# Performer attention with a gated MLP on one core: w_out loaded in eight pieces, and 120 scheduling priorities shifted by a search

## The chip, the core and the metric

The kernel runs on one core of one Trainium2 chip. The core has TensorE for matmuls ("PE" in the profile, and "PEld" for its weight loads), VectorE (DVE), ScalarE (ACT), GpSimd (POOL) and SyncE (SP), which here issues loads and stores. The metric is the device time of one execution in microseconds. An execution with a profile also has a span, from the first to the last instruction; in nearly all executions here the time is 1.8 to 2.1 us longer than the span.

## The reference, cut to what matters

```python
# q, k, v: (8 batches, 8 heads, 576 rows, 64) f32;  omega: (128, 64)
def phi(x):                                   # random features
    h = einsum('bhsd,md->bhsm', x, omega) - sum(x*x)/2
    return exp(h - max(h)) / sqrt(m)
kv  = einsum('bhsm,bhsd->bhmd', phi(k), v);  z = sum(phi(k), axis=2)
x   = einsum('bhsm,bhmd->bhsd', phi(q), kv) / (einsum(phi(q), z) + 1e-6)
x   = x as (4608, 512)
h   = x @ w_in                                # (512, 2048)
out = (h * clip(h + 3, 0, 6) / 6) @ w_out     # (2048, 512)
```

## The kernel before: the parts that the change touches

The kernel is written as a list of operations, each with a priority, the buffers it reads and writes, and an assumed duration on each engine that may do it. A list scheduler in the Python program plays this list against its own model of the core. Out of that come a fixed order of instructions for each engine, a choice of engine where there is one, and the semaphore waits. The chip keeps to this order (all 2233 weight loads stand in the same order in the three traces of the changed kernel), so an order that fits the model and not the chip costs time.

There are three stages. Attention of batch 0 runs alone (the "head"). Then TensorE does the first layer of block b beside the attention of batch b+1. The second layer of block b follows one block later. While TensorE has nothing to do in the head, dummy matmuls on a tile `fill` keep it busy.

```python
W_GATE = [("vl", 0)]*2+[("v32", 1, 3)]*2       # what each of four w_in loads waits for
...
def w_out_piece(g, gate):                      # four loads of 512 rows, cast to bf16 on the way
    op("POOL", 2.95, lambda E: E.dma_start(
        wo[:, 4 * g:4 * g + 4, :], w_out[512 * g:512 * g + 512, :].rearrange("(c p) e -> p c e", p=128)),
       -0.2 + 0.05 * g, reads=gate, writes=[("wo", g)], ...)
...
# scaling of the 64 leftover rows of v ("vcl"), one op for each half of the partitions;
# it reads the landed rows ("vl") and reciprocals of the first k maxima ("cc", "l")
op(EV_V if b else V0, {"POOL": 0.62, "DVE": dvet(260)}, ... E.tensor_tensor(vcl..., vl..., cc..., ALU.mult), ...)
...
# transposes on PE go to a PSUM bank of a ring of eight; a copy by DVE or ACT frees the bank
op("PE", len(dbl) * 0.057, e_T, p, reads=..., writes=[vT], alloc=[vT], ...)
op(EV_T if b else T0, both(n, 2), evac(... dst ..., ... vT ...), p, reads=[vT], writes=[(t + "T", x) for x in dbl])
...
def mm2(blk, tc):                              # second layer: 16 matmuls in groups of four
    for g in range(4):
        def e(E, g=g, ...):
            for f in range(4 * g, 4 * g + 4):
                ins = E.matmul(ring.t[vo.slot][...], gT[gu][:, f, 128 * tc:128 * tc + 128], wo[:, f, c0:c1], ...)
        op("PE", 4 * mmt(w), e, t, reads=[("gT", ...)...] + [("wo", g)], writes=[vo], alloc=[vo] if g == 0 else [], ...)
...
load(2, (), {"k": [("wo", 1)], "q": [("wo", 2)], "v": [("wo", 3)]})   # loads of batch 2 wait for w_out
```

The softmax here doesn't subtract the row's maximum and nothing guards it: scores larger than these inputs give would overflow.

## Time and profile before

The first three executions took 323.71 to 324.29 us, median 324.18. In rough numbers, of the profiled execution (span 321.8 us):

| stretch (us) | what PE does | lost there |
|---|---|---|
| 0 to 17.3 | head: attention of batch 0, 63 dummy matmuls | about 11.4 us |
| 17.3 to 38.95 | first layer of block 0, attention of batch 1 | about 0.3, before 18 us |
| 38.95 to 40.0 | changes over to the second layer | 0.6 to 0.7 |
| 40.0 to 318.8 | both layers, attention of later batches | 0 |
| 318.8 to 321.8 | last copy and store | not on PE |

"Lost" is PE's time that is not spent on real matmuls. Reading a trace in this way takes one more step than reading its busy shares, because a dummy is busy too. I take the weight loads in order of time and pair them with the program's own order of matmuls. Each matmul then counts for its start-to-start time at full rate in this trace (0.2158 us for 512 columns, 0.1093 for 256, 0.032 for 65, and so on), and a dummy counts for nothing. The loss at a moment is the time since the span's start minus the work done so far. Weight loads run ahead of their matmuls (by 0.21 us for most in this trace), so a value is good to about 0.15 us.

### The profile page before, as it was taken

How to read it: one execution, taken by the hardware profiler on the slowest of the kernel's cores; microseconds unless marked ns; L12 is line 12 of the kernel's file. 1: busy time of each engine (PE TensorE's matmuls, PEld its weight loads, DVE VectorE, ACT ScalarE, POOL GpSimd, SP SyncE). 2: the span in 40 equal slices, each digit the busy share in tenths (PEclk: the TensorE clock that was granted, in tenths of full speed). 3: DMA queues.
4: the chain of work that ended last, by engine and by line, in shares of the span. 5: the costliest groups of instructions: out<-in, count | busy, mean ns of one | idle time of the engine just before them, and what ended most of it. 6: DMA issues, size and time to landing. Idle time of an engine off the chain costs nothing.

```text
span 321.8 us, 5873 instructions
## 1 busy us (share of the span) xinstructions
PE 317.0 (98%) x2236; PEld 174.8 (54%) x2236; DVE 209.0 (65%) x460; ACT 189.1 (59%) x385; POOL 76.8 (24%) x107
## 2 busy tenths in 40 slices
PE   8999999999999999999999999999999999999996
PEld 6789855455654544565555545555555444444443
DVE  4988985597787947995796478846866353433411
ACT  3996982596595516966775387647674254344400
POOL 2765171065040600730333022402020000000000
DMA  7999999999940999897829963998012201000024
GB/s 249 269 201 204 236 146 234 225 184 170 226 122 34 136 173 271 99 196 118 236 31 188 191 208 39 183 201 224 16 50 67 73 27 41 33 35 33 33 67 98
DMA packets 91532, 44.79 MB, mean 139 GB/s; under 512 B 58096, under 2 KB 87024, under 8 KB 91504
## 3 DMA queue, kind: packets, MB, share of 16 engines
q1 hardware_dynamic: 64288, 31.31, 42.1%
q0 software_dynamic: 26512, 12.46, 31.4%
q10 hardware_dynamic: 704, 0.66, 0.6%
q8 instruction: 18, 0.29, 0.4%
q14 instruction: 10, 0.08, 0.1%
HBM read 36.73 MB, written 9.44 MB: 143 GB/s over the span
## 4 chain that ended last, share of the span: by engine, by line
PE 94%; DVE 4%; POOL 1%; issue 0%; ACT 0%; POOLq 0%; DVEq 0%
PE p L917 39%; PE p L859 34%; PE p L656 5%; PE p L639 4%; PE p L884 4%; PE p L791 3%; PE p L763 2%; DVE mx L648 2%; PE p L466 2%; PE p L429 1%; PE p L765 1%; POOL vc L750 0%; DVE vc L750 0%; DVE vcl L679 0%; DVE gT L895 0%
## 5 line engine op out<-in xcount | busy, mean ns | idle before, releaser
L917 PE MATMUL p<-wo,gT 128*128 128x512 bf16 (+2 forms) x592 | 141.0, 373 | 0.3 <-DVE qT L418 0.3
L867 DVE SCALAR_TENSOR_TENSOR gT<-tsb,p 128x512 bf16<-128x512 bf16 x128 | 86.8, 685 | 56.7 <-ACT tsb L865 56.1
L865 ACT ACTIVATE tsb<-p 128x512 bf16<-128x512 f32 x128 | 76.3, 601 | 71.1 <-PE p L859 70.6
L859 PE MATMUL p<-xT,wi 128*128 128x512 bf16 x448 | 107.3, 379 | 0.0
L917 PEld LDWEIGHTS p<-wo,gT 128*128 128x128 bf16 x592 | 56.1, 98 | 57.5 <-DVE qT L418 0.5
L859 PEld LDWEIGHTS p<-xT,wi 128*128 128x128 bf16 x448 | 42.6, 98 | 45.4
L648 DVE TENSOR_REDUCE mx<-kp 128x4 f32<-128x512 bf16 x72 | 46.7, 674 | 9.7 <-ACT kp L645 9.4
L645 ACT ACTIVATE kp<-p 128x512 bf16<-128x512 f32 x72 | 40.0, 619 | 15.1 <-PE p L639 15.1
L660 ACT ACTIVATE qpT<-p 128x512 bf16<-128x512 f32 (+1 forms) x80 | 41.4, 575 | 4.8 <-PE p L656 4.6
L750 POOL TENSOR_TENSOR vc<-v,cc 128x512 bf16<-128x512 f32 x22 | 23.4, 1064 | 36.3 <-DVE cc L746 27.0
L807 DVE TENSOR_TENSOR xb<-p,rec 128x384 bf16<-128x384 f32 (+1 forms) x64 | 28.5, 477 | 0.0
L639 PE MATMUL p<-om,kT 128*128 128x256 bf16 x144 | 23.0, 273 | 0.0
L656 PE MATMUL p<-qT,om 128*128 128x512 bf16 (+1 forms) x80 | 22.8, 358 | 0.0
L418 DVE COPY osb<-p 128x512 f32<-128x512 f32 (+2 forms) x12 | 7.8, 647 | 22.7 <-PE p L917 22.7
L417 ACT COPY osb<-p 128x512 f32<-128x512 f32 x25 | 14.8, 591 | 11.3 <-PE p L917 11.3
L500 POOL DMA_DIRECT2D k<-in_k_dram x12 | 9.1, 767 | 41.9 <-PE p L859 33.7
L639 PEld LDWEIGHTS p<-om,kT 128*128 128x128 bf16 x144 | 13.8, 98 | 9.7
L791 PEld LDWEIGHTS p<-kvz,qpT 128*128 128x128 bf16 x312 | 13.5, 98 | 5.8 <-ACT qpT L660 0.2
L859 PE MATMUL p<-xS,wi 128*128 128x512 bf16 x64 | 16.4, 379 | 0.0
L884 PE MATMUL p<-xT,wi 128*128 128x256 bf16 x128 | 15.9, 272 | 0.0
L763 PEld LDWEIGHTS p<-vc,kp 128*128 128x128 bf16 x256 | 11.9, 98 | 6.1 <-POOL vc L750 0.4
L791 PE MATMUL p<-kvz,qpT 128*128 128x65 bf16 x312 | 14.8, 194 | 0.0
(69 smaller groups left out, 215.9 us busy)
## 6 DMA issues: line engine op xcount, KB each, us to landing
out_dram<-osb SPq DMA_DIRECT2D x32, 256.0 KB, 2.6
v<-in_v_dram SPq DMA_DIRECT2D x14, 512.0 KB, 5.3
wi<-in_moe_w_in_dram POOLq DMA_DIRECT2D x4, 512.0 KB, 8.3
k<-in_k_dram POOLq DMA_DIRECT2D x8, 256.0 KB, 5.1
k<-in_q_dram POOLq DMA_DIRECT2D x8, 256.0 KB, 6.2
wo<-in_moe_w_out_dram POOLq DMA_DIRECT2D x4, 512.0 KB, 12.8
kb<-in_k_dram POOLq DMA_DIRECT2D x6, 256.0 KB, 5.3
qb<-in_q_dram POOLq DMA_DIRECT2D x6, 256.0 KB, 7.6
```

What stands on the lines that cost most here:

```text
L639: ins = E.matmul(ring.t[vK.slot][:, 256 * i:256 * i + 256], kT[:, 2 * u + i, :], om[:].rearrange("d t m -> d (t m)"), start=True, stop=True)
L645: op("ACT", actt(512), lambda E, u=u, vK=vK: E.activation(kp[pb][:, 4 * u:4 * u + 4, :].rearrange("p c m -> p (c m)"), ring.t[vK.slot], AF ...
L648: op("DVE", dvet(512), lambda E, u=u: E.reduce_max(mx[pb][:, 4 * u:4 * u + 4], kp[pb][:, 4 * u:4 * u + 4, :], axis=AX.X), pos(u) + 0.03, r ...
L656: op("PE", mmt(n), lambda E, vQ=vQ, lh=lh: E.matmul(ring.t[vQ.slot][:, 0:n], om[:, lh, :], src, start=True, stop=True), p + 0.045 * lh, re ...
L660: op("ACT", actt(n), lambda E, vQ=vQ, lh=lh: E.activation(dst(lh), ring.t[vQ.slot][:, 0:n].rearrange("m (j t) -> m j t", t=128), AF.Exp, s ...
L791: ins = E.matmul(d[:, hh, i - i0, :], qpT[pb][:, o:o + 128], kvz[m][:, 65 * hh:65 * hh + 65], start=True, stop=True)
L807: op("DVE", dvet(128 * n), lambda E: E.tensor_tensor(xv(i0, i1), psum()[:, :, :, 0:64], rbc, ALU.mult), t + 0.01, reads=[vn, ("rec", ru)], ...
L859: ins = E.matmul(ring.t[vh.slot], wi[:, c, 128 * f:128 * f + 128], xv[:, c, :], start=(c == 0), stop=(c == NJ - 1))
L865: op("ACT", actt(512), lambda E: E.activation(tsb[tu][:], ring.t[vh.slot], AF.Relu, bias=0.5, scale=1.0 / 6.0), t - 0.1, reads=[vh], write ...
L867: op("DVE", dvet(512), lambda E: E.scalar_tensor_tensor(gT[gu][:, f, :], tsb[tu][:], 1.0, ring.t[vh.slot], ALU.min, ALU.mult), t - 0.1, re ...
L884: ins = E.matmul(ring.t[vh.slot][:, 256 * g:256 * g + 256], wi[:, c, 128 * (f + g):128 * (f + g) + 128], xT[0][:, c, 256 * half:256 * half ...
L917: ins = E.matmul(ring.t[vo.slot][:, 0:c1 - c0], gT[gu][:, f, 128 * tc:128 * tc + 128], wo[:, f, c0:c1], start=(f == 0), stop=(f == NF - 1))
```

## The change

`URGENT` and `FIT` are two tolerances, in us, with which the scheduler picks the next instruction, and `NUDGE` is added to the priorities of the operations with these numbers. The intent is to let the second layer start on half a piece of w_out, and to find a better order of the first two batches by a search that shifts priorities and keeps what shortens the scheduler's own model.

```diff
-URGENT = 0.8
-FIT = 0.05
+URGENT = 0.5
+FIT = 0.1
+NUDGE = {
+    114: 0.0222, 119: 0.0169, 120: 0.0216, 122: 0.0313, 123: 0.0172, 124: -0.0176, 134: -0.0037, 137: 0.0668,
+    138: -0.1599, 142: -0.1553, 143: -0.0153, 145: 0.0442, 146: -0.0653, 147: -0.0395, 149: -0.042,
     ... (120 operations in all)
-    if idle and (not cand or idle[0][0] + (0.02 if idle[0][0] < 8.0 else idle[0][1].occ) <= m):
+    if idle and (not cand or idle[0][0] + (0.02 if idle[0][0] < 4.8 else 0.2 if idle[0][0] < 8.0 else idle[0][1].occ) <= m):
-    W_GATE = [("vl", 0)]*2+[("v32", 1, 3)]*2
+    W_GATE = [("q32", 1, 3)] * 4
+    WO = [(2 * i, 2 * i + 2) for i in range(8)]
     def w_out_piece(g, gate):
-        op("POOL", 2.95, lambda E: E.dma_start(
-            wo[:, 4 * g:4 * g + 4, :], w_out[512 * g:512 * g + 512, :].rearrange("(c p) e -> p c e", p=128)),
+        f0, f1 = WO[g]
+        op("POOL", 0.7375 * (f1 - f0), lambda E: E.dma_start(
+            wo[:, f0:f1, :], w_out[128 * f0:128 * f1, :].rearrange("(c p) e -> p c e", p=128)),
     ... (assumed GpSimd times of two scalings raised: 0.62 to 0.72, 1.2 to 1.32)
-            for g in range(4):
+            for f0, f1 in WO if blk == 0 else [(4 * g, 4 * g + 4) for g in range(4)]:
     ... (block 0 takes its second layer in groups of two matmuls, each waiting for its piece)
-            load(2, (), {"k": [("wo", 1)], "q": [("wo", 2)], "v": [("wo", 3)]})
+            load(2, (), {"k": [("wo", 4)], "q": [("wo", 5)], "v": [("wo", 7)]})
+    for i, x in NUDGE.items():
+        G.ops[i].prio += x
     G.schedule()
```

Lines move by 20 to 26: L429 of before (transposes) is L449 after, L859 is L882, L917 is L941.

## The prediction

> **What bounds the kernel now.** I first read the busy shares and the slices of the page. TensorE (PE) is the only engine that is full, from the second slice to the last:
>
> ```profile
> span 321.8 us, 5873 instructions
> PE 317.0 (98%) x2236; PEld 174.8 (54%) x2236; DVE 209.0 (65%) x460; ACT 189.1 (59%) x385; POOL 76.8 (24%) x107
> PE   8999999999999999999999999999999999999996
> ...
> DMA  7999999999940999897829963998012201000024
> ```
>
> 98% busy does not yet mean that nothing can be gained, because the kernel holds dummy matmuls on `fill` (line 466), which count as busy. So the second view is the busy time by stretches, once for all work and once for line 466 alone:
>
> ```profile
> 0.00:17.30 17.30, 15.98 (x154) 12.37 (x155) 12.50 (x38) 12.08 (x27) 9.48 (x18) 1.00 1.00 256
> 17.30:38.95 21.65, 21.57 (x253) 19.04 (x250) 18.56 (x46) 17.85 (x38) 9.03 (x14) 1.00 1.29 214
> 38.95:40.00 1.05, 0.65 (x9) 0.30 (x7) 1.04 (x3) 1.05 (x4) 0.97 (x2) 1.00 1.23 205
> 40.00:318.80 278.80, 278.79 (x1830) 143.08 (x1830) 176.65 (x374) 158.09 (x319) 57.27 (x76) 1.00 0.69 126
> 318.80:321.80 3.00, 0.00 (x0) 0.00 (x0) 0.29 (x1) 0.00 (x0) 0.00 (x0) 1.00 0.42 102
> ```
>
> (columns: stretch, length, then busy us and instructions of PE, PEld, DVE, ACT, POOL, the granted clock, the DMA share, GB/s.) The reader is to see four parts. Up to 17.3 us PE is mostly on dummies: the same stretch for line 466 alone gives 10.85 us. From 17.3 to 38.95 it never waits for long. Around 39 there is one hole. From 40.0 to 318.8 it is packed. Then 3.0 us of last eviction and store follow.
>
> Third, to be sure that "packed" is not an illusion of overlapping matmuls, I took the step from one matmul's start to the next. For 512 columns it is 0.216 us, for 256 columns 0.1094 us, for 65 columns 0.032 us. Counting all non-dummy matmuls at those steps gives, as an estimate, 1136 x 0.216 + 288 x 0.109 + 576 x 0.032 + some 11 us for the other shapes = about 306 us. PE runs from 1.3 to 318.8, which is 317.5 us. So about 11.5 us in all are not real work: some 10.8 in the first 17.3 us, and 0.73 in the hole at 39. No reordering can touch the 306 us. This is the ceiling of what the change can give, and I don't expect more than a small part of it, since the first inputs must land and attention of batch 0 must run before dense work exists.
>
> Fourth, the chain of waits in the head. It leaves PE at 8.05 and comes back at 17.6:
>
> ```profile
> 8.70 2.96 DVE mx L648 x5
> 12.59 1.19 DVE mx L648 x2
> 14.37 1.08 DVE mx L648 x2
> 16.20 1.37 POOL vc L750
> ```
>
> VectorE is at work without a break from 7.0 to 17.1 (4.00 of 4.00 us between 12 and 16), ScalarE as well between 12 and 16, and the last piece is a scaling of v on GpSimd (POOL) that stands behind a cast (15.50 to 16.12), which stands behind two issues of w_in loads:
>
> ```profile
> 10.62 1.70 POOL L476 DMA_DIRECT2D wi<-in_moe_w_in_dram  x2 [1.06 <-DMA vl<-in_v_dram]
> 12.33 1.43 POOL L679 TENSOR_TENSOR vcl<-vl,cc 64x260 bf16<-64x260 f32 x2
> 13.90 1.55 POOL L476 DMA_DIRECT2D wi<-in_moe_w_in_dram  x2
> ```
>
> So the head is bounded by three vector engines working in a bad order, and GpSimd sits still for 1.06 us only because the first w_in load is gated on the landing of the leftover rows of v.
>
> **What the Trainium skill says.** "TensorE: Matmul & The Clock Gate", section "Wait — 56ns, not 53.3ns?", gives the warm start-to-start time as N/2.4 GHz plus about 2.5 ns, 215.7 ns for 512 columns. The trace has 0.216 us, so the 279 us of packed stretch run at the array's rate. "Perfetto Trace Analysis", section "Identifying the Most-Contended Engine", says that matmul busy time is no good measure of headroom; that is why I counted steps. Here it agrees in one sense (10.85 busy us are dummies) and otherwise the packed part has none to give. "DMA: Bandwidth & Descriptors", section "Issuing engines are not separate DMA queues", says all DMAs run on the same 16 engines and interleave; the trace agrees: the four w_out loads are issued 0.74 us apart and land 10.4, 11.9, 13.7 and 15.5 us after issue, thus one every 2.3 to 2.5 us (38.3, 40.6, 43.2, 45.7). Each reads 1 MB of f32, so the stream moves about 0.4 MB per us and is full. Cutting it into eight pieces cannot make the last byte earlier; it only tells PE earlier of the first half of each piece.
>
> **The change part by part.**
>
> *w_out in eight pieces.* Four issues of 0.76 us become eight. An issue of 64 KB or 256 KB costs GpSimd about the same 0.75 us (three k loads took 2.30), so GpSimd pays 4 x 0.75 = 3.0 us more, between 28 and 34. It has nothing to do from 30.96 to 38.58 (its wait there is 7.62 us), so the cost on the path is 0. The gain: the first rows are usable half a piece, 1.2 us, earlier (about 37.1 rather than 38.3), and each later half as well. That is worth something only at the hole at 39. There PE finished its transposes, and the first w_out matmuls started at 39.98 on the release of a PSUM buffer by a VectorE copy. I give 0.5 of the 0.73 us to the change.
>
> *w_in gated on the landing of q instead of v.* The last q load lands at 9.75 (issue 4.27, 5.5 us), the leftover v at 10.3. GpSimd's first two casts of q end at 9.56. So the four issues can run from 9.8 to 13.0 without a gap, instead of 10.62 to 12.32 and 13.90 to 15.45. The scaling of the leftover v slides from 12.33 to about 13.0, but the cast and the last scaling (15.50 to 17.57) can move up by about 1.0 us, if VectorE delivers its reductions as early. Against that, w_in joins the DMA stream 0.85 us earlier while v is still landing (11.1 to 13.6), on full DMA engines, so v comes perhaps 0.4 us later and w_in as a whole only about 0.4 us earlier.
>
> *Dummies and priorities.* From 4.8 to 8 us of the scheduler's own clock, a dummy is placed only into a hole of over 0.2 us, not 0.02. In the trace a dummy takes 0.213 us until about 6.3 us, twice what the scheduler assumes for most of them, and the first real transposes start at 5.24 behind six dummies though their cast ended at 4.44. Thinning them gives 0.2 to 0.4 us at the start of the chain. The shifted priorities lie nearly all in attention of batch 0 and 1 (numbers 114 to 430), none in the packed part where they would matter. The largest concern the leftover k rows (their copy, their projection) and the exponentials after them, i.e. what ScalarE and VectorE do between 5 and 9 us, when ScalarE is idle for 0.81 and 1.49 us. Moving copies there from VectorE can shorten VectorE's unbroken 10 us by one or two copies of 0.37 us.
>
> *Sum.* The head: the last scaling up to 1.0 us earlier on GpSimd, and VectorE 0.5 to 1.0 us earlier; the later of both counts, so I take 0.9. The hole: 0.5. New waits from a schedule that the chip does not follow to the tenth: +0.2. Total -1.2 us. Because the orders were searched for, and the model's target is just this head, I add 0.3. 324.2 - 1.5 = 322.7 us.
>
> **The rivals.** (1) *The head's gain is given back at 38 to 45 us.* PE would run out of first-layer matmuls a microsecond earlier, while the DMA stream, full from the first slice to 45 us, delivers w_out only 0.4 us earlier. For it: DMA shares of 1.2 to 1.5 in these stretches. Against it: half pieces make the first rows usable 1.2 us earlier, and once a piece is there it feeds four token tiles for 3.4 us while the next needs 2.5. It would leave 323.8. (2) *v or w_in becomes the bound of the head*: half A of the first layer reaches the last w_in piece at about 26.1 and that lands at 24.8, so 1.3 us of slack; v later by over 1 us would hold the scalings. That makes 324.5 to 325. (3) *The search found much more*, such as starting the first layer 3 us earlier: 320.5. Against it: first k at 3.8 us, last v at 13.6, and 10 us of VectorE work in between.
>
> **Range and chances.** The median of 324.18 has a spread of 0.6 over its three runs. With the head worth 0 to 2.5 and the hole -0.7 to +0.7, I take 321.0 to 324.2. Two per cent are 6.5 us, over half of all that is not real work (11.5), and nothing in the DMA order allows it: 0.02 for faster. Slower by 6.5 us would need PE to lose it in a packed stretch whose order hardly changes: 0.02.
>
> **What would show it.** After: PE's real work unchanged and 2236 matmuls less or more a few dummies; the last dummy at about 16 rather than 17 us; all four w_in issues together near 10 us; the first matmul of the first layer near 18.5 rather than 19.4; the hole at 39 gone or under 0.3 us; eight w_out issues of 0.75 us with GpSimd idle after them; the packed stretch shifted by 1 to 2 us as a block and the same 3.0 us after the last matmul. I am wrong if the head is shorter but a new hole of over 0.5 us stands between 35 and 47 us, or if PE waits again after 60 us.

## The result

The changed kernel took 322.82 us median (322.39 to 323.25, four executions), against 324.05 (323.71 to 324.29, four) for the kernel before. The ratio is 0.9963, 95% interval 0.9944 to 0.9982, which is still clear of 1. A ratio here is the mean time of one kernel's executions over that of the other's in the same rounds, so it is not quite the ratio of the medians.

The changed kernel was run 15 times (median 322.89) and the kernel before 53 times (median 323.84). The gain is about 1.0 us.

The page of the changed kernel, first lines:

```profile
span 321.2 us, 5834 instructions
PE 313.5 (98%) x2198; PEld 173.8 (54%) x2233; DVE 208.2 (65%) x459; ACT 190.2 (59%) x384; POOL 80.1 (25%) x113
```

There is a trap in the second line. PE has 2198 matmuls but 2233 weight loads, while before had 2236 of each. Three dummies fewer are real (60 instead of 63). The other 35 are records of matmuls that the trace lacks, and each shows as about 0.05 us in which PE seems idle (a matmul of 512 columns is recorded as 0.379 us long, so its neighbours cover most of its step of 0.216). The view by stretches shows it too: after 40 us "busy" of PE is 1.8 us short of the stretch, where before was full, while PEld is unchanged.

```profile
17.30:38.95 21.65, 21.65 (x258) 19.21 (x255) 19.36 (x51) 18.57 (x41) 12.72 (x20) 1.00 1.30 213
38.95:40.00 1.05, 1.00 (x10) 0.57 (x9) 1.05 (x3) 1.05 (x4) 0.80 (x1) 1.00 1.24 205
40.00:318.20 278.20, 276.41 (x1799) 143.03 (x1831) 175.20 (x371) 159.49 (x319) 56.90 (x76) 1.00 0.71 127
```

What is to be seen is the second line, PE at 1.00 of 1.05 us, where before had 0.65. The hole at 39 is gone. The timeline of weight loads, where no records are missing, says how. Before (start, length, what; the bracket is the idle time ahead of it and who ended it):

```profile
38.12 0.88 PEld L429 LDWEIGHTS p<-ident,k 128*128 128x128 bf16 x14
39.28 0.23 PEld L429 LDWEIGHTS p<-ident,k 128*128 128x128 bf16 x4 [0.28 <-ACT kp L645]
39.97 0.55 PEld L917 LDWEIGHTS p<-wo,gT 128*128 128x128 bf16 x4 [0.46 <-DVE qT L418]
```

The changed kernel:

```profile
38.29 0.77 PEld L449 LDWEIGHTS p<-ident,k 128*128 128x128 bf16 x12
39.01 0.58 PEld L941 LDWEIGHTS p<-wo,gT 128*128 128x128 bf16 x4
39.71 0.54 PEld L449 LDWEIGHTS p<-ident,k 128*128 128x128 bf16 x6
```

Before, PE made 18 transposes in a row and then wanted a bank for the first w_out matmul. That matmul reads only `gT` and `wo`, so a wait for the copy of `qT` can only be a wait for the PSUM bank which that copy frees. The copies came late: ScalarE was in a run of eight exponentials until 39.2, and VectorE did the leftover scaling first.

```profile
38.62 0.87 DVE L679 TENSOR_TENSOR vcl<-vl,cc 64x260 bf16<-64x260 f32 x1
39.50 0.95 DVE L418 COPY qT<-p 128x512 bf16<-128x512 bf16 x3
```

After the change, four w_out matmuls stand between the 12th and the 13th transpose and give the copies 0.86 us. The leftover scaling also comes five microseconds earlier (GpSimd's half starts at 33.67 and VectorE's at 33.81, where before had 38.58 and 38.62), so VectorE's copies of `qT` start at 38.82.

The head of the profiled execution is another matter. The chain of waits of the changed kernel between 12 and 15 us:

```profile
12.43 0.13 DVE vc L773
12.56 0.53 issue
13.09 1.27 DVE mx L671 x2
14.37 0.02 issue
14.39 0.44 DVE vcl L702
14.82 0.05 issue
14.87 0.43 PE p L786 x8
```

and its GpSimd timeline, to be held against the one in the prediction:

```profile
10.58 3.18 POOL L496 DMA_DIRECT2D wi<-in_moe_w_in_dram  x4 [0.51 <-DMA q<-in_q_dram]
13.75 0.66 POOL L702 TENSOR_TENSOR vcl<-vl,cc 64x260 bf16<-64x260 f32 x1
14.49 2.35 POOL L773 TENSOR_TENSOR vc<-v,cc 128x512 bf16<-128x512 f32 x2
```

The four issues do run in a row, as intended. But they start at 10.58, as late as before (10.62), because in this execution the last q load landed at 10.27 and not at 9.75. They push the scaling of the leftover v from 12.33 to 13.75 (and its other half, on VectorE, to 14.39). The first matmuls with v wait for that. PE's loss by 38 us is 11.83 here and 11.66 in the trace of before. A single pair of traces would thus say that the whole gain is the hole and the new head a small loss. The experiments showed that one pair of traces cannot carry this reading of the head.

### The profile page after: what moved, and what is told of

Read it like the earlier page. It is cut to its first block, busy times and chain, and to the rows that moved or that the text cites. A ratio compares the mean times of both kernels' runs of the same rounds, so it can differ in the third digit from the quotient of the medians.

```text
span 321.2 us, 5834 instructions
## 1 busy us (share of the span) xinstructions
PE 313.5 (98%) x2198; PEld 173.8 (54%) x2233; DVE 208.2 (65%) x459; ACT 190.2 (59%) x384; POOL 80.1 (25%) x113
## 4 chain that ended last, share of the span: by engine, by line
PE 92%; DMA 2%; SPq 2%; ACT 2%; issue 1%; DVE 1%; DVEq 0%; ACTq 0%
PE p L941 38%; PE p L882 33%; PE p L907 4%; PE p L662 4%; PE p L679 4%; PE p L814 3%; PE p L786 2%; DMA v<-in_v_dram 2%; SPq L523 2%; PE p L449 1%; ACT qpT L683 1%; ACT tsb L888 1%; PE p L788 1%; DVE mx L671 0%; DVE gT L890 0%
## 5 line engine op out<-in xcount | busy, mean ns | idle before, releaser
L941 PE MATMUL p<-wo,gT 128*128 128x512 bf16 (+2 forms) x574 | 138.7, 373 | 0.9
L882 PE MATMUL p<-xT,wi 128*128 128x512 bf16 x436 | 105.8, 379 | 0.7
L941 PEld LDWEIGHTS p<-wo,gT 128*128 128x128 bf16 x592 | 56.3, 98 | 58.0
L882 PEld LDWEIGHTS p<-xT,wi 128*128 128x128 bf16 x448 | 42.9, 98 | 46.6
L773 POOL TENSOR_TENSOR vc<-v,cc 128x512 bf16<-128x512 f32 x23 | 24.3, 1055 | 35.4 <-DVE cc L769 26.1
L679 PE MATMUL p<-qT,om 128*128 128x512 bf16 (+1 forms) x76 | 22.0, 357 | 0.1
L702 POOL TENSOR_TENSOR vcl<-vl,cc 64x260 bf16<-64x260 f32 x8 | 5.0, 620 | 49.4 <-DVE cc L698 49.2
L882 PE MATMUL p<-xS,wi 128*128 128x512 bf16 x63 | 16.4, 379 | 0.1
```

The source lines that it names most:

```text
L679: op("PE", mmt(n), lambda E, vQ=vQ, lh=lh: E.matmul(ring.t[vQ.slot][:, 0:n], om[:, lh, :], src, start=True, stop=True), p + 0.045 * lh, re ...
L882: ins = E.matmul(ring.t[vh.slot], wi[:, c, 128 * f:128 * f + 128], xv[:, c, :], start=(c == 0), stop=(c == NJ - 1))
L941: ins = E.matmul(ring.t[vo.slot][:, 0:c1 - c0], gT[gu][:, f, 128 * tc:128 * tc + 128], wo[:, f, c0:c1], start=(f == 0), stop=(f == NF - 1))
```

## The experiments

Twelve kernels were run, five rounds each. Those of one call shared their runs of the kernel before, whose medians were 323.87, 323.95, 323.68 and 323.69 us in the four calls, which ran on more than one chip. The losses of PE in each trace, from the weight loads as described above, are the common yardstick:

```text
kernel          clock full  last q landed  lost by 38  hole (55 minus 38)  lost by 300
before             6.5          9.75         11.66          +0.62            12.12
before_again       4.4          9.50         11.35          +0.57            11.75
pieces_only        4.2          9.74         11.63          +0.25            11.71
old_head           5.5          9.90         11.76          -0.13            11.88
belief10           4.4         10.08         11.89          -0.01            11.70
v_pool_before      6.5          9.87         12.01          +0.63            12.47
after              4.0         10.27         11.83          -0.13            11.53
after_again        6.9          9.64         12.18          -0.13            11.89
after_third        4.4         10.86         12.47          -0.13            12.17
no_pieces          7.1          9.78         12.33          +0.01            12.18
beliefA10          4.2         10.89         12.46          -0.11            12.79
v_pool_after       7.0         10.35         11.90          -0.13            11.59
head_only          5.8          9.70         11.31          +0.57            11.71
old_gate           4.0          9.88         12.03          -0.12            12.96
```

All in us; "clock full" is the moment at which a matmul of 256 columns goes from 421 to 273 ns in the trace, and its step from 0.213 to 0.109 us. "-0.13" is no hole, it is the yardstick's reading error. The first six have the old head, the next seven the new one, and old_gate a mixture.

### after_again and before_again: the two kernels once more

No edit. They give a second trace and the spread of the times.

> The changed kernel unaltered, for a second trace and for its spread. Its four times were 322.39, 322.50, 323.14 and 323.25, and its trace is of the 323.14 execution, in which the fourth k load landed at 6.62 us where the trace of before has 6.16. Theory A (the gain is the hole at 39 us alone): again about 1.2 us under before at the median only by chance of the draw; in the trace PE time not spent on real work stands at 11.7 to 11.9 us by 38 us, as in before, and grows by less than 0.1 across 39. Theory B (the reordered head gains too, and the profiled execution drew late first loads): an execution with k landing near 6.2 us shows 11.0 to 11.3 us lost by 38 us.

Measured: 322.85 us median (322.42 to 323.35), ratio 0.9967 (0.9950 to 0.9984). The gain repeats. The trace, of the slowest of the five executions, has 12.18 us lost by 38 us with the k load at 6.07 us, which neither theory expected. So the fourth k load alone does not decide.

> The kernel before unaltered, as a null: ratio 1.000 within 0.002, 323.7 to 324.3 us, 11.6 to 11.9 us of PE lost by 38 us and 0.6 to 0.7 more in the hole at 39 us. Both theories expect the same; if the loss in the head differs by over 0.3 us from the first trace of before, a single trace of the head cannot be compared with another.

Measured: 323.79 us (323.34 to 324.12), ratio 0.9994 (0.9978 to 1.0010), a clean null. The loss by 38 us is 11.35, or 0.3 less than in the first trace of the same kernel, and the hole is 0.57. So the hole is firm, while the head varies by execution, and one trace of it cannot be compared with another.

### pieces_only: the eight pieces alone

```diff
-        op("POOL", 2.95, ... four loads of 512 rows
+        f0, f1 = WO[g]
+        op("POOL", 0.7375 * (f1 - f0), ... eight loads of 256 rows, groups of two matmuls in block 0, gates 4, 5, 7
```

> Before with w_out in eight pieces, everything else as it was (the same 63 dummies). Theory A: the hole at 39 us goes (under 0.1 us), the head is that of before, so 0.5 to 0.7 us faster, ratio 0.998. Theory B: the pieces give at most half of the gain; 0.6 of 1.2 us as well, so here the theories only part on no_pieces. Rival C (the pieces are worth nothing, the hole goes by order alone): ratio 1.000 and the hole stays at 0.6 us.

Measured: 323.72 us median, but in two groups: 322.99, 323.13, 323.26 and 324.17, and two at 325.06 and 325.58. Ratio 1.0009 (0.9981 to 1.0036), so the times don't settle it. In the trace the hole shrinks from 0.6 to 0.25 us: four w_out matmuls now stand after the 8th transpose, and PE still waits once for a bank afterwards. Executions near 325 occur in before (325.45, 325.20) and in the changed kernel (325.22) as well; what makes them is open.

### no_pieces: the changed kernel with four pieces

```diff
-    WO = [(2 * i, 2 * i + 2) for i in range(8)]      # and groups of two, gates 4, 5, 7
+    ...four loads of 512 rows, groups of four, gates 1, 2, 3 as before (priorities renumbered to match)
```

> The changed kernel with w_out in four pieces again, shifted priorities, gates and thresholds kept. Theory A: the hole at 39 us is back at 0.5 us or more and nothing of the gain is left, ratio to before 0.999 to 1.001. Theory B: half of the gain stays, 0.5 to 0.7 us under before, ratio 0.998.

Measured: 323.69 us (322.70 to 324.10), ratio 0.9989 (0.9972 to 1.0005). Theory A was wrong about the hole. The order is again 18 transposes in a row, and yet the trace has no hole:

```profile
38.79 1.12 PEld L448 LDWEIGHTS p<-ident,k 128*128 128x128 bf16 x18
39.87 0.58 PEld L936 LDWEIGHTS p<-wo,gT 128*128 128x128 bf16 x4
```

In this kernel the shifted priorities alone had the leftover scaling start at 34.17 (GpSimd) and 34.31 (VectorE), and put a pair of k projections at 31.56 us instead of among the last six. VectorE's copies of `qT` start at 39.33 with no scaling of the leftover v just before them. So there are two cures for the hole: something for PE to do between transposes, and an earlier end of the other engines' work. The changed kernel has both. The fourteen traces agree: where the leftover scaling starts at 38.2 us or later and the 18 transposes stand in a row, the hole is there (before twice, head_only, v_pool_before, 0.57 to 0.63); where it starts at 33.7 to 34.7, there is none.

### old_head and head_only: the change cut in two

```diff
 # old_head: the changed kernel with the head of before
+URGENT = 0.8; FIT = 0.05; W_GATE, threshold and costs of before; NUDGE only for numbers from 260 on
 # head_only: the changed kernel with four pieces
+NUDGE only for numbers under 260
```

> The changed kernel with everything that acts on batch 0 put back (thresholds, gates of w_in, costs, the 56 priorities numbered under 260), the eight pieces and the other priorities kept. Four traces so far, paired by when the clock is released (near 4.2 or near 6.7 us), say: the new head loses 0.5 us more than the old by 38 us, the hole gives 0.7 to 0.8 back. Theory A (all gain from the hole, the head a loss): PE lost by 38 us 11.3 to 11.7, hole under 0.2, 322.3 to 322.7 us, so 0.3 to 0.5 faster than the changed kernel. Theory B (the head gains in most executions, the traced ones were unlucky): 323.2 to 323.5, 0.5 slower than the changed kernel.

Measured: 323.32 us (322.98 to 323.60), ratio 0.9978 (0.9966 to 0.9990). That is 0.7 us better than before, and there is no hole. Its median is about 0.4 above the changed kernel's, but from another call, and the ratios (0.9978 here; 0.9963, 0.9967 and 0.9986 there) have intervals that overlap. Theory A, that the new head is a loss, had forecast 322.3 to 322.7 and missed; the time is that of theory B (323.2 to 323.5). The trace loses another 0.4 us between 85 and 105 us, in a wait for a copy by ScalarE. (The text above says 56 priorities under 260; the list has 44.)

> The other half: the head of the changed kernel, w_out in four pieces, no other priority shifted. Theory A: lost by 38 us 11.8 to 12.3 and the hole at 39 to 40 us takes up to 0.3 more where the head came early, 0 where it came late; 0.2 to 0.4 slower than before, 324.1 us. Theory B: 0.5 faster than before, 323.4.

Measured: 323.52 us (323.23 to 324.51), ratio 0.9991 (0.9978 to 1.0004). The hole is there, 0.57. Its head is the best of all traces, 11.31 us lost by 38 us, with the same order of PE up to 27 us as the traces that lost 11.8 to 12.2. By its time of 323.52 this run fits theory B (323.4) better than theory A (324.1), and it gave the key. Its last q load landed at 9.70, and its w_in issues began at 10.01 instead of 10.58, and everything up to the first matmul with v came 0.57 us earlier with them:

```profile
10.01 3.18 POOL L486 DMA_DIRECT2D wi<-in_moe_w_in_dram  x4 [0.52 <-DMA q<-in_q_dram]
13.17 0.66 POOL L689 TENSOR_TENSOR vcl<-vl,cc 64x260 bf16<-64x260 f32 x1
```

With that column in the table the head can be read. In the new head, "lost by 38" minus "last q landed" is 1.56 (after), 1.61 (head_only), 1.55 (v_pool_after), 1.61 (after_third) and 1.57 (beliefA10). In the old one it is 1.91, 1.85, 1.89, 1.86 and 1.81, and 2.14 in v_pool_before. So where the landing of q decides, the new head is 0.3 us shorter, 1.58 against 1.86. The three traces of the changed kernel had q late twice (10.27, 10.86); four of the seven new-head traces have it later than any old-head trace, and whether that is chance is not shown.

Two new-head traces don't fit: after_again and no_pieces have 2.54 and 2.55. The traces show where it goes. VectorE comes to its half of the leftover scaling, the last thing before the first matmul with v, after GpSimd has begun its own scaling of v, and then takes more than twice as long. In after_again, and for comparison in head_only:

```profile
13.84 1.04 POOL L774 TENSOR_TENSOR vc<-v,cc 128x512 bf16<-128x512 f32 x1
14.09 1.07 DVE L703 TENSOR_TENSOR vcl<-vl,cc 64x260 bf16<-64x260 f32 x1
...
13.81 0.43 DVE L689 TENSOR_TENSOR vcl<-vl,cc 64x260 bf16<-64x260 f32 x1
13.91 2.36 POOL L760 TENSOR_TENSOR vc<-v,cc 128x512 bf16<-128x512 f32 x2
```

It took 1.07 and 1.11 us in these two traces, and 0.42 to 0.43 in the five others, where VectorE was first by 0.04 to 0.10 us. In the two, VectorE was late because an earlier scaling of v took 1.10 and 1.09 us instead of 0.69 to 0.75; why is not shown. Against the 1.86 of the old head the new one thus won 0.3 us in five traces and lost 0.7 in two. Over all traces the loss beyond the landing of q averages 1.86 us in the new head and 1.91 in the old, so a gain by the head is not shown.

### old_gate: the changed kernel with the old gate of w_in

```diff
-    W_GATE = [("q32", 1, 3)] * 4
+    W_GATE = [("vl", 0)]*2+[("v32", 1, 3)]*2
```

> The changed kernel with the w_in loads gated on v again. If the four issues in a row on GpSimd are what delays the scaling of the leftover v (13.75 and 14.39 us, with PE idle 0.6 to 0.9 us before it), the idle time of PE at 14 to 15 us goes and 0.3 to 0.6 us less is lost by 38 us; 322.4 us. If the delay comes from the shifted priorities or late v loads, the hole at 14 us stays and the time with it, 322.8 or more, since the priorities were searched for the other gate.

Measured: 323.49 us (322.96 to 324.73), ratio 0.9991 (0.9974 to 1.0008). The head is no better. GpSimd's half of the leftover scaling came earlier (12.45), but VectorE's half still at 13.94. PE began the first matmuls with v at 14.42, 4.54 us after q landed, where the changed kernel has 4.60. The loss by 38 us is 2.15 over the landing of q, as much as in the worst trace of the old head (2.14). In this trace the shifted priorities without their gate are no gain. The traced execution lost another microsecond much later, in the stretch that I had called packed:

```profile
160.57 0.31 PEld L786 LDWEIGHTS p<-vc,kp 128*128 128x128 bf16 x8 [1.22 <-POOL vc L773]
```

GpSimd and VectorE had waited there for a load of v, which landed at 158.9.

### belief10: four loads, but the order of eight

```diff
-            for g in range(4):                       # groups of four
+            for f0, f1 in [(2 * i, 2 * i + 2) ...]:  # groups of two in block 0, each waiting for its 512 rows
-           ... group="dwo%d" % g, inc=16, lat=1.0
+           ... group="dwo%d" % g, inc=16, lat=0.0    # the model believes in a landing 1 us earlier
```

Only the scheduler's belief changes; the loads and what is waited for stay those of before. Its order of PE is that of before up to the 12th transpose at 39 us.

> Before with w_out in four loads, but the first rows of the second layer taken two matmuls at a time and the scheduler told that w_out lands 1 us earlier than it assumed; the loads and waits are those of before. The order at 39 us becomes that of the changed kernel (12 transposes, 4 w_out matmuls, 6 transposes). Order theory: w_out's first 512 rows land at 38.3 to 38.4 us anyway, PE reaches them at 38.8, so the hole is under 0.2 us and the time that of pieces_only without its outliers, 323.2 to 323.5. Landing theory (half pieces are needed on the chip): PE waits for the load at 38.5 to 39.5 us, later pieces hold it too (40.6, 43.2, 45.7), 0.3 us or more lost, 324 us.

Measured: 323.06 us (322.71 to 324.17), ratio 0.9978 (0.9961 to 0.9994). The hole is gone without any smaller load; the first 512 rows landed at 38.83 us, 0.26 before PE took them:

```profile
38.35 0.77 PEld L429 LDWEIGHTS p<-ident,k 128*128 128x128 bf16 x12
39.09 0.57 PEld L918 LDWEIGHTS p<-wo,gT 128*128 128x128 bf16 x4
```

### beliefA10: the same in the changed kernel

```diff
 # no_pieces, plus
-           groups of four; lat=1.0
+           groups of two; lat=0.0
```

> The changed kernel with w_out in four loads of 512 rows, its matmuls still two at a time and the scheduler told that w_out lands 1 us earlier, so that the order at 39 us stays mixed (12 transposes, then w_out matmuls and transposes in turn). Order theory (after belief10): no hole, the time of the changed kernel, 322.6 to 323.1 us, 0.996 to 0.998 of before. Landing theory: a wait of PE for w_out of 0.3 us or more near 39 us and 323.5 or more.

Measured: 324.11 us (322.86 to 324.63), ratio 0.9998 (0.9976 to 1.0020). The mechanism held: no hole in the trace, though the first 512 rows landed only at 39.18 us, because PE reached them at 39.92. The time did not hold. In the traced execution q landed at 10.89, and 0.4 us more were lost near 150 us. Another of the six had 3.3 us outside its span (one of no_pieces had 2.6). Four loads in the changed kernel (no_pieces and this one) stay behind eight by more than their traces explain, and I leave that open.

### v_pool_before and v_pool_after: v issued by GpSimd

```diff
+            pool = cast or (b > 2 and part[0] == "v")
-            e = "POOL" if cast else eng[...] ... else "SP"
+            e = "POOL" if pool else eng[...] ... else "SP"
```

> Before with the loads of v for batches 3 to 7 issued by GpSimd instead of SyncE, where they stand behind the transposing loads; PE's order is the same to the end of batch 1. In the traces v of batches 5 to 7 is waited for on landing (margin 0.0 to 0.1 us), and in old_gate one such landing 2 us later cost PE 1.2 us at 156 to 161 us. Late-v theory: the executions at 324.0 to 324.5 us are such cases; with the loads issued earlier they go, median 323.4 or less, ratio 0.998 or less, spread under 0.5. Rival (the spread is made in the head, by late first loads and by when the clock is released): the median stays within 0.2 of before's and the spread with it. Third: GpSimd issues them no earlier, or its own work comes later, and it is slower.

Measured: 324.51 us (323.95 to 325.03, one slow execution left out), ratio 1.0014 (0.9995 to 1.0033). The third way: the loads for batch 5 were issued 1.2 us earlier (148.9 against 150.1 in before_again) and landed 2.3 us later (158.6 against 156.3). The late-v theory of the spread isn't supported, and since nothing landed earlier it isn't refuted either. In its head two scalings again took longer (GpSimd's first half of the leftover rows 1.14 us, elsewhere in the old head 0.73 to 0.75; VectorE's first scaling of v 1.04, elsewhere 0.69 or 0.70), which goes with its 2.14.

> The same in the changed kernel. Late-v theory: it has less of this (batch 5 has 3 to 4 us of margin, batch 6 has 0.1), so it gains less: 322.4 to 322.8 us against 322.8. Rival: 322.8, no gain. If both gain it is the fastest kernel of the study. Its trace is one more sample of the new head: by 38 us 11.3 to 12.3 us lost, as in the four so far.

Measured: 323.68 us (322.70 to 325.66), ratio 0.9995 (0.9966 to 1.0024). The spans are mostly 320.6 to 321.3 as in the changed kernel, but 2.1 to 2.9 us of the time lie outside the span instead of 1.8 to 2.1. It beats nothing.

### after_third: the changed kernel a third time

No edit.

> The changed kernel a third time, for one more trace and five more times. Nine executions so far span 320.5 to 321.5 us, in two groups (320.5 to 320.8 and 321.2 to 321.5), and both traces are of the upper group. Theory: the groups differ in the head. A trace of the lower group must show 11.2 to 11.4 us of PE lost by 38 us (head_only, with the same order of PE to 27 us, showed 11.31), no hole at 39 us and nothing after 60; one of the upper group 11.8 to 12.2 by 38 us. Rival: the groups differ in the packed stretch, so a trace of the lower group still shows 11.8 or more by 38 us and the upper ones lose it later.

Measured: 323.00 us (322.57 to 325.22), ratio 0.9986 (0.9961 to 1.0010); without the execution at 325.22 the times are 322.57 to 323.66. The trace is of the 323.66 execution: q landed at 10.86 and 12.47 us are lost by 38 us. The loss is 12.17 by 300 us, so it was made in the head, as the theory of the two groups says. A trace of the fast group was not to be had: the traced execution is the first of each series, and all three were in the slower half of theirs.

## Why the prediction was right, and where it was not

**The total.** 322.7 was predicted and 322.82 measured; the gain was put at 1.5 and is 1.0 to 1.2 us. That the time came so near is partly luck: the sum started from 324.2, where 53 executions of the kernel before give 323.84, and this offset hid part of the gain's excess. Of the terms, the head was put too high at 0.9, the new waits did not come, and the 0.3 added for the search stood for nothing that was seen.

**What bounds the kernel** held. The list of real matmuls is the same. The loss before 38 us and the hole are the only places in which the traces of the two kernels differ. One correction is needed: "packed" is not safe against everything. In old_gate one late load of v cost PE 1.2 us at 160 us, and old_head and beliefA10 each lost 0.4 us after 55 us.

**The hole.** I gave it 0.5 us; it is worth about 0.6 to 0.7 (0.57 to 0.63 in four traces that have it, none in the three of the changed kernel; old_head and belief10, which have the old head and no hole, are both at 0.9978, or 0.7 us). The step named the right wait, a PSUM bank, but the wrong cure. That "the first rows are usable half a piece, 1.2 us, earlier" is not what helps. belief10 shows it: four loads, no hole. In the changed kernel the four matmuls at 39.01 read two pieces, of which the second landed at 38.33, and before's first 512 rows landed at 38.34. What the smaller pieces did was to make the scheduler's model place the first w_out matmuls between transposes, and the shifted priorities moved other engines' work out of the way (no_pieces).

**w_in gated on q.** The step was right in direction and over in size. At equal landing of q, the last scaling ends 7.12 us after it (17.39 minus 10.27) and before 7.81 (17.56 minus 9.75), so 0.7 earlier where I had "about 1.0". The slide of the first half of the leftover scaling, which I put at 0.7, is 0.9 (3.48 us after q against 2.58). The first matmul with v comes 4.60 us after q instead of 4.06 (14.87 and 13.81), and PE idles in the meantime. What is left in the loss is 0.3 us in the five traces where q decides, and nothing on the average of all seven, where the sum had 0.9 for the head. The mis-sized term is this one. What it left out is that GpSimd's and VectorE's scalings now stand side by side, and in two traces VectorE's half took 1.1 us instead of 0.4. head_only's ratio of 0.9991 would be a gain of 0.3 us, but its interval reaches past 1.

**Dummies and priorities.** Three dummies fewer, as allowed for; the last one starts near 16.7 instead of 17.0 us, not near 16, and the first matmul of the first layer at 19.1 instead of 19.4, not near 18.5. Thinning was not tried alone. Of the 120 shifted priorities 91, and not nearly all, have numbers from 114 to 430. **New waits**, +0.2: none found in the traces of the changed kernel after 38 us.

**The eight issues** cost 0.73 us each and fall between 27.2 and 35.0, where GpSimd has little else; nothing waits for them, so their cost on the path is 0 as said. All w_out loads are issued by GpSimd, so their landing one after another fits what I cited on issuing engines but does not test it.

**The rivals.** The first, that the head's gain is given back at 38 to 45 us, did not come: the loss by 55 us follows the loss by 38 one to one, with the hole as a constant of 0.6 in before. The second, v or w_in as the bound, came in a shape that I had not seen: in most traces q's landing became the bound of the head. The third did not come.

By what the runs show the hole is worth 0.6 to 0.7 us of the 1.0 to 1.2 measured. The rest may be the head, but that is not shown: old_head and belief10, with the old head and no hole, stand at 0.9978, within the intervals of the changed kernel. And three kernels with the new head and no hole gained less (no_pieces 0.9989, v_pool_after 0.9995, beliefA10 0.9998), which stays open.

## What to carry to other kernels

A hole on the bound engine can be closed by order alone: before making a transfer smaller, look whether the data was already there when the engine stood, and which buffer it stood for. When two traces of a few-microsecond stage are compared, find the event that it hangs on (here the landing of one load) and compare from there; otherwise the scatter of that event, 1.4 us here, buries an effect of 0.3. And look at the traces that don't fit before setting them aside: here they showed a cost of the new order.

## What the Trainium skill lacked or had wrong

- "Perfetto Trace Analysis", which recommends the busy share of weight loads over that of matmuls: it should add that matmul records can be missing, here 35 of 2233 in one trace, each looking like about 0.05 us of idle PE, while the weight loads were complete.
- "DMA: Bandwidth & Descriptors" has no figure for the scatter of one and the same load between executions: the fourth q load, issued at 4.3 us in all traces, landed between 9.50 and 10.89 us, and in ten of the thirteen traces with an old or a new head the loss by 38 us followed it at a distance fixed for each head to within 0.1 us (1.81 to 1.91 old, 1.55 to 1.61 new).
- "TensorE: Matmul & The Clock Gate" (Part 1) puts the transition to full rate at about 4 us into sustained matmul activity, give or take 500 ns between runs. In these fourteen traces it came at 4.0 to 7.1 us of the span, with the first matmul at 1.3 us, so 2.7 to 5.8 us in. The half-rate step of 0.213 us for 256 columns agrees with the page.
